# Fused attention and two MLPs on one core: first eight chunks of q and k in four groups of two, tau and the first weight pieces asked for later

## The chip, the cores and the metric

One core of one Trainium2 chip. The metric is device time in microseconds (us) of one execution. The kernel before takes 1052.99 us (median of 3 runs, 1052.94 to 1054.34). The engines are called as in the profile: PE (TensorE), DVE (VectorE), ACT (ScalarE), POOL (GpSimd) and SP, which here only asks for transfers.

## The reference

```python
qn = q / (norm(q, axis=1) + 1e-6)          # q, k, v: 1 x 6080 x 256
kn = k / (norm(k, axis=1) + 1e-6)
s  = kn.T @ qn / tau                       # 256 x 256
a  = softmax(s, axis=-1)
x  = v @ a                                 # 6080 x 256
h  = x @ w_in;  g = max(0.01 * h, h);  x = g @ w_out
h  = x @ w2_in; g = where(h >= 1, h, where(h <= -1, 0, (h + 1)**2 / 4))
out = g @ w2_out                           # w_in 256 x 2048, w_out 2048 x 256
```

[...]

## The kernel before

**Stage 1 (the loop over `groups`, lines 353 to 384)** reads q and k once, in groups of 128-row chunks: two groups of two chunks, ten of four, one of two, and a rest of 2 x 96 rows. Per group SP asks for q and for k (line 357), PE adds the group's part of kn.T @ qn into PSUM (`s_matmuls`, line 350: four matmuls of 256 columns per chunk pair, that is two per chunk), ACT squares both tiles and DVE adds the squares into `accq` and `acck` (line 373; the first two groups are squared straight into the two halves of the accumulators, line 368, and need no add). For the last four groups (`HELD`) PE takes one half of the columns at once and the other half after the loop. Then come the norms (`nq`, `nk`), the softmax and its transposes.

**The weights** come in 32 *pieces* of 512 KB, in the order of `pieces`: w_in 0, w_in 1, w_out 0, w_in 2, w_out 1, and so on. `load_pieces` asks for one; `LOAD_AT` names the groups of stage 1 after which one more is asked for, by ACT's queue. `decode_piece` turns float64 bits into float32: ACT makes the magnitude (`magnitude`, line 180), DVE works on it (lines 193, 195, 198, 202, 206) and adds the parts (210, 213 or 229). From w_in 2 and w_out 0 on, ACT then copies the sum into a rounded high part (lines 220, 237) and DVE subtracts for the low part (217, 233).

**The order of the work** is written out by hand. `decode_piece` is a generator: `pump(n)` takes as many of its steps as `n` credits pay for, between other instructions. What ACT has to do for a piece isn't issued by the generator: it is put on a list (`later`), and `flush()` issues that list. Inside stage 1 there are a flush and a pump per tile; a piece isn't touched before two groups after the one it was asked for (`loaded_at[i] + 2 > group[0]`). Behind stage 1 `FLUSH` and `PUMP` give the places, in slots of one PE product:

```python
PUMP = [..., ((0.8, 2.4, 3.9, 5.4, 6.6, 8.6, 10.0), 2.6), ((1.4, 2.8, 5.4, 6.9, ...), 2.6)]
FLUSH = [..., (0.5, 2.0, 3.5), (0.5, 1.4, 4.4, 5.3, 11.8, 14.8, 15.7)]
```

The second entries hold for the first eighth of the first layer, which lasts 10.5 slots; the third for the other seven. So the flushes there are at slots 0.5, 2.0, 3.5 and then at 10.5 + 0.5 = 11.0.

**Stage 2, the first layer's first pair of column blocks**, uses the weights as they get ready. In eighth j, PE multiplies x by the product wx of softmax and w_in j (tile `ph`, lines 331 to 333: high x high, low x high, high x low), ACT takes the leaky relu `c` (600) and rounds it to `gh` (618), DVE makes `gl` (623), and PE multiplies by w_out j (tile `acc`, reads `l2w`, high part in 331, low part in 332). One `wps` product per eighth makes the next wx from `et` and w_in j + 1 (reads `w1i`: high part in 331 and 332, low part in 333). PE, ACT and DVE each run their instructions in the order issued.

**Transfers**: a transfer signals one of eight semaphores (DMAHW0 to 7) that go round among all transfers of SP and ACT. Whoever asks with a number waits until the transfer that had that number last has landed.

Of the kernel before, what the change touches and what calls it, by code (L numbers as in the profile page):

```python
# [11 lines left out]
AF = mybir.ActivationFunctionType  # L12
# [10 lines left out]
CPG = 4  # L23
WARM = 8
HELD = 4


A11, A22, A12, S1, S2, S3, S4 = range(7)
# [33 lines left out]
        ((3, 6.0), (4, 6.0), (5, 6.0), (6, 6.0), (7, 6.0), (7, 10.9), (7, 16.0))]  # L62


LOAD_AT = (1, 2, 4, 8)
FOLD = 12

PLAIN_W = 2

# [7 lines left out]
def xcit_moe_moe(ctx, tc, q, k, vT, tau, w_in, w_out, w2_in, w2_out, outT):  # L77
# [10 lines left out]
    nc = tc.nc  # L88
    V, G, A = nc.vector, nc.gpsimd, nc.scalar
# [36 lines left out]
    def flush():  # L126

        while later:
            later.pop(0)()

    def load_pieces(n, dma):

        while len(raws) < min(n, len(pieces)):
            nm, j = pieces[len(raws)]
            if nm[-1] == "o":
                src = weights[nm].rearrange("(k p) c w -> p k c w", p=P)[:, 2 * j:2 * j + 2]
            else:
                src = weights[nm].rearrange("(k p) f w -> p k f w", p=P)[:, :, 256 * j:256 * (j + 1)]
            raw = dec.tile([P, 2, 256, 2], U32, tag="raw", name="raw", bufs=3)
            dma.dma_start(out=raw, in_=src)  # L140
            loaded_at[len(raws)] = group[0]
            raws.append(raw)
# [130 lines left out]
    def pump(n):  # L273
        nonlocal credit
        credit = min(credit + n, 2 * n)
        while credit > 0:
            c = next(prep)
            if c == 100:
                break
            credit -= c  # L280
# [24 lines left out]
    half, tiny, dummy = (const.tile([P, 1], F32, name=nm) for nm in ("half", "tiny", "dummy"))  # L305
    ones = const.tile([P, P], F32, name="ones")
    ident = const.tile([P, P], F32, name="ident")
    tau_sb = const.tile([P, 1], F32, name="tau_sb")
# [4 lines left out]

    groups = []
    t0 = 0
    for s in [2, 2] + [CPG] * 10 + [2]:
        groups.append((t0, P, s))
        t0 += P * s
    groups.append((t0, (N - t0) // 2, 2))
# [19 lines left out]
    for _ in range(WARM):  # L339
        nc.tensor.matmul(out=warm, lhsT=ones, rhs=ones, start=True, stop=True)  # L340

    A.activation(out=dummy, in_=tiny, func=AF.Sqrt)
    nq = ps_h.tile([P, NB], F32, tag="h", name="nq")[:, :C]
    nk = ps_h.tile([P, NB], F32, tag="h", name="nk")[:, :2 * KC].rearrange("p (c t) -> p c t", c=KC)
    tiles = []
# [1 line left out]
    def s_matmuls(ic, gi):  # L347
        kt, qt, rows, s = tiles[gi]
        for i in range(s):
            nc.tensor.matmul(out=s_ps[ic], lhsT=kt[:rows, i, ic * P:(ic + 1) * P], rhs=qt[:rows, i, :],  # L350
                             start=gi == 0 and i == 0, stop=gi == len(groups) - 1 and i == s - 1)

    for gi, (t0, rows, s) in enumerate(groups):
        tl = []
        for src, nm in ((q, "q"), (k, "k")):
            t = ep.tile([P, CPG, C], F32, tag=nm, name=nm)
            nc.sync.dma_start(out=t[:rows, :s, :], in_=src[t0:t0 + rows * s, :].rearrange("(p s) c -> p s c", s=s))
            tl.append(t)
        if gi == 0:
            nc.sync.dma_start(out=tau_sb, in_=tau)  # L360
        qt, kt = tl
        tiles.append((kt, qt, rows, s))
        s_matmuls(0, gi)
        if gi < len(groups) - HELD:
            s_matmuls(1, gi)
        for t, a in ((qt, accs[0]), (kt, accs[1])):
            if gi < 2:
                A.activation(out=a[:, 2 * gi:2 * gi + 2, :], in_=t[:, :s, :], func=AF.Square)
            else:
                sq = ep.tile([P, CPG, C], F32, tag="sq", name="sq", bufs=4)  # L370
                A.activation(out=sq[:rows, :s, :], in_=t[:rows, :s, :], func=AF.Square)
                if gi < FOLD:
                    V.tensor_add(out=a, in0=a, in1=sq)
                else:
                    for i in range(0, s, 2):
                        V.tensor_add(out=a[:rows, 0:2, :], in0=a[:rows, 0:2, :], in1=sq[:rows, i:i + 2, :])
            if gi == FOLD - 1:
                V.tensor_add(out=a[:, 0:2, :], in0=a[:, 0:2, :], in1=a[:, 2:4, :])
            flush()
            if gi < len(groups) - 4:  # L380
                pump(S_PUMP)
        group[0] = gi
        if gi in LOAD_AT:
            load_pieces(min(len(raws) + 1, decoded[0] + 3), A)
    xr = load_x(0, 0, nc.sync)
# [2 lines left out]

    for gi in range(len(groups) - HELD, len(groups) - HELD + 2):
        s_matmuls(1, gi)  # L390
    for i in range(2):
        nc.tensor.matmul(out=nq, lhsT=ones, rhs=accs[0][:, i, :], start=i == 0, stop=i == 1)
    for ic in range(KC):
        for i in range(2):
            nc.tensor.matmul(out=nk[:, ic], lhsT=accs[1][:, i, ic * P:(ic + 1) * P], rhs=ones[:, :2], start=i == 0, stop=i == 1)
    for gi in range(len(groups) - HELD + 2, len(groups)):
        s_matmuls(1, gi)
# [274 lines left out]
    for i, (m, p, j) in enumerate(quads):  # L672
# [7 lines left out]
        t = base  # L680
# [21 lines left out]
        if m == 0:  # L702
            k = 0 if not first else 2 if i else 1
# [4 lines left out]
        if j == 0 and i + NQ < len(quads):  # L708
            nm, np_, _ = quads[i + NQ]
# [9 lines left out]
    for k in range(4 * KC):  # L719
        t = base + 2 + k  # L720
# [35 lines left out]
```

## Time and profile before

| what | value |
|---|---|
| runs | 1054.34, 1052.99, 1052.94 us |
| profiled execution, first to last instruction (span) | 1052.2 us; no other time of it is given |
| PE / DVE / ACT busy | 99% / 77% / 80% |
| granted clock of PE, mean | 1.000 |
| stage 1, from the first S matmul to the norms | 4.27 to 47.06 us |
| first product with w_out 0 | 65.70 us |

A row of the timeline has start, duration, engine, line, operation, written tile <- read tiles, and in brackets how long the engine had been idle and what ended it. A float32 matmul is two records. Times are microseconds from the start of the span.

### The profile page before, as it was taken

What the parts mean: (1) busy time and instruction counts of PE and PEld (TensorE: products, weight loads), DVE (VectorE), ACT (ScalarE), POOL (GpSimd) and SP (SyncE); (2) the same over time, 40 slices, a digit from 0 to 9 for tenths busy, and PEclk for the clock granted to TensorE, in tenths of its full rate; (3) what the DMA queues carried; (4) which work ended last, traced back from release to release, by engine and by line L of the source; (5) the groups of instructions that cost most, each with busy time, mean ns of one, the idle gap of its engine ahead of it and who ended that gap; (6) DMA issues with size and microseconds to landing.
All of it is one profiled execution on the core that took longest, in us unless ns stands there. A gap on an engine that the chain in (4) does not pass through costs nothing.

```text
span 1052.2 us, 13435 instructions
## 1 busy us (share of the span) xinstructions
PE 1042.1 (99%) x4676; PEld 870.3 (83%) x4676; DVE 814.6 (77%) x1366; ACT 837.0 (80%) x1437; POOL 0.9 (0%) x9
## 2 busy tenths in 40 slices
PE   8999999999999999999999999999999999999998
PEld 7888878888888887888888888888888888888887
DVE  5989887678778778876547779779778878878765
ACT  6677777777787777777668888888888888888886
POOL 0000000000000000000000000000000000000000
PEclk9999999999999999999999999999999999999999
DMA  9645465448759569556446445436435444543531
GB/s 355 240 168 165 158 250 200 165 160 295 256 196 329 181 229 319 204 202 223 150 165 208 145 152 204 165 115 224 157 136 196 159 165 168 185 147 129 205 140 63
DMA packets 54164, 201.82 MB, mean 192 GB/s; under 512 B 5520, under 2 KB 6544, under 8 KB 54096
## 3 DMA queue, kind: packets, MB, share of 16 engines
q1 hardware_dynamic: 53008, 198.86, 53.9%
q10 hardware_dynamic: 1088, 2.10, 0.5%
q8 instruction: 37, 0.61, 0.2%
q14 instruction: 31, 0.25, 0.1%
HBM read 163.32 MB, written 37.62 MB: 191 GB/s over the span
## 4 chain that ended last, share of the span: by engine, by line
PE 95%; DMA 2%; DVE 1%; ACT 1%; issue 0%; SPq 0%; DVEq 0%
PE acc L332 16%; PE acc L333 16%; PE acc L331 16%; PE pX L331 7%; PE pX L332 7%; PE pX L333 7%; PE pW L331 4%; PE pW L333 4%; PE pW L332 4%; PE s_ps L350 4%; PE pY L332 2%; PE pY L333 2%; PE pY L331 2%; PE ph L332 1%; PE ph L331 1%; PE ph L333 1%
## 5 line engine op out<-in xcount | busy, mean ns | idle before, releaser
L623 DVE TENSOR_TENSOR gl<-c,gh 128x512 fp32r<-128x512 f32 (+1 forms) x384 | 261.0, 680 | 65.7 <-ACT gh L618 65.1
L332 PE MATMUL acc<-gh,l2w 128*128 128x512 f32 (+1 forms) x768 | 297.6, 387 | 0.2 <-DVE l2w L233 0.2
L331 PE MATMUL acc<-gh,l2w 128*128 128x512 f32 (+1 forms) x768 | 297.5, 387 | 0.0
L333 PE MATMUL acc<-gl,l2w 128*128 128x512 f32 (+1 forms) x768 | 297.5, 387 | 0.0
L618 ACT CAST gh<-c 128x512 fp32r<-128x512 f32 (+1 forms) x384 | 234.9, 612 | 5.3 <-DVE c L614 0.8
L332 PEld LDWEIGHTS acc<-gh,l2w 128*128 128x128 f32 x768 | 144.1, 188 | 28.9 <-DVE l2w L233 0.5
L331 PEld LDWEIGHTS acc<-gh,l2w 128*128 128x128 f32 x768 | 144.1, 188 | 28.8 <-ACT l2w L237 0.3
L333 PEld LDWEIGHTS acc<-gl,l2w 128*128 128x128 f32 x768 | 144.1, 188 | 28.6
L331 PE MATMUL pX<-xo,l1w 128*128 128x512 f32 (+1 forms) x352 | 136.3, 387 | 1.2 <-ACT s L583 1.2
L605 ACT ACTIVATE u<-c,half 128x512 f32<-128x512 f32 (+1 forms) x144 | 103.8, 721 | 42.1 <-DVE c L591 42.0
L332 PE MATMUL pX<-xo,l1w 128*128 128x512 f32 (+1 forms) x352 | 136.3, 387 | 0.0
L333 PE MATMUL pX<-xo,l1w 128*128 128x512 f32 (+1 forms) x352 | 136.2, 387 | 0.0
L583 ACT COPY s<-pX 128x512 f32<-128x512 f32 (+1 forms) x176 | 101.6, 577 | 30.1 <-PE pX L333 30.1
L608 ACT ACTIVATE u<-u 128x512 f32<-128x512 f32 (+1 forms) x192 | 120.6, 628 | 1.3
L600 ACT ACTIVATE c<-c 128x512 f32<-128x512 f32 (+1 forms) x120 | 75.2, 627 | 55.8 <-DVE c L591 55.5
L591 DVE TENSOR_TENSOR c<-pY,s 128x512 f32<-128x512 f32 (+1 forms) x88 | 60.2, 684 | 61.8 <-PE pY L333 57.1
L614 DVE SCALAR_TENSOR_TENSOR c<-u,c 128x512 f32<-128x512 f32 (+1 forms) x144 | 98.1, 681 | 10.6 <-ACT u L608 10.6
L591 DVE TENSOR_TENSOR c<-pW,s 128x512 f32<-128x512 f32 (+1 forms) x88 | 60.3, 685 | 39.3 <-PE pW L333 28.6
L591 DVE TENSOR_TENSOR c<-pX,s 128x512 f32<-128x512 f32 (+1 forms) x88 | 60.2, 684 | 24.3 <-PE pX L333 20.8
L331 PEld LDWEIGHTS pX<-xo,l1w 128*128 128x128 f32 x352 | 66.1, 188 | 14.8 <-ACT s L583 1.6
L332 PEld LDWEIGHTS pX<-xo,l1w 128*128 128x128 f32 x352 | 66.1, 188 | 13.1
L333 PEld LDWEIGHTS pX<-xo,l1w 128*128 128x128 f32 x352 | 66.1, 188 | 13.1
(123 smaller groups left out, 1315.0 us busy)
## 6 DMA issues: line engine op xcount, KB each, us to landing
l1w<-l1d SPq DMA_DIRECT2D x80, 896.0 KB, 4.6
l2w<-l2d SPq DMA_DIRECT2D x88, 512.0 KB, 5.1
raw<-in_w_out_dram SPq DMA_DIRECT2D x15, 512.0 KB, 5.9
l1d<-l1w SPq DMA_DIRECT2D x8, 896.0 KB, 4.4
l1d<-l1s SPq DMA_DIRECT2D x8, 896.0 KB, 5.3
raw<-in_w_in_dram SPq DMA_DIRECT2D x13, 512.0 KB, 6.1
q<-in_q_dram SPq DMA_DIRECT2D x10, 512.0 KB, 8.0
k<-in_k_dram SPq DMA_DIRECT2D x10, 512.0 KB, 9.1
```

The costliest lines, as they stand in the source:

```text
L331: nc.tensor.matmul(out=out, lhsT=wh, rhs=mh, start=first, stop=False, skip_group_check=skip)
L332: nc.tensor.matmul(out=out, lhsT=wl, rhs=mh, start=False, stop=False, skip_group_check=skip)
L333: nc.tensor.matmul(out=out, lhsT=wh, rhs=ml, start=False, stop=last, skip_group_check=skip)
L350: nc.tensor.matmul(out=s_ps[ic], lhsT=kt[:rows, i, ic * P:(ic + 1) * P], rhs=qt[:rows, i, :], start=gi == 0 and i == 0, stop=gi == len(gro ...
L583: A.copy(out=s[i], in_=bank["W" if i == "5" else "X"])
L591: V.tensor_tensor(out=tile_c(r), in0=bank[name], in1=s[i], op=ALU.add)
L600: A.activation(out=c[r], in_=src, func=AF.Prelu, alpha=0.01)
L605: A.activation(out=u[r], in_=source(r), func=AF.Relu, scale=0.5, bias=half[:, 0:1])
L608: A.activation(out=u[r], in_=u[r], func=AF.Square)
L614: V.scalar_tensor_tensor(out=c[r], in0=u[r], scalar=1.0, in1=src, op0=ALU.min, op1=ALU.max)
L618: A.copy(out=g[int(r[0]), int(r[1])][0], in_=c[r])
L623: V.tensor_tensor(out=lo, in0=c[r], in1=hi.bitcast(F32), op=ALU.subtract)
```

## The change

Stage 1 now has four groups of two chunks at its start (`SMALL`) and nine of four; its groups are numbered one higher from there on, and the place where the accumulators are folded (`FOLD`) moves with them. Groups 2 and 3 are squared into a tile and added by DVE in halves of the accumulators. ACT asks for the first k, SP for all else of q and k. tau is asked for by ACT after group 3 and no longer by SP after the first k. The square-root call that loads ACT's table stands after the squares of group 0. The first four weight pieces are asked for after groups 3, 4, 6 and 9 of the new count, in place of 1, 2, 4 and 8: in chunks read by then, 8, 12, 20 and 32 in place of 4, 8, 16 and 32.

```diff
+SMALL = 4
-LOAD_AT = (1, 2, 4, 8)
-FOLD = 12
+LOAD_AT = (3, 4, 6, 9)
+FOLD = 13
-    for s in [2, 2] + [CPG] * 10 + [2]:
+    for s in [2] * SMALL + [CPG] * 9 + [2]:
-    A.activation(out=dummy, in_=tiny, func=AF.Sqrt)
-            nc.sync.dma_start(out=t[:rows, :s, :], in_=src[...])
+            (A if gi == 0 and nm == "k" else nc.sync).dma_start(out=t[:rows, :s, :], in_=src[...])
-        if gi == 0:
-            nc.sync.dma_start(out=tau_sb, in_=tau)
-                if gi < FOLD:
+                if gi < SMALL:
+                    V.tensor_add(out=a[:, 2 * gi - 4:2 * gi - 2, :], in0=a[:, 2 * gi - 4:2 * gi - 2, :], in1=sq[:, 0:2, :])
+                elif gi < FOLD:
                     V.tensor_add(out=a, in0=a, in1=sq)
+        if gi == 0:
+            A.activation(out=dummy, in_=tiny, func=AF.Sqrt)
         group[0] = gi
+        if gi == LOAD_AT[0]:
+            A.dma_start(out=tau_sb, in_=tau)
         if gi in LOAD_AT:
             load_pieces(min(len(raws) + 1, decoded[0] + 3), A)
```

What moves, in three places. First, ACT behind stage 1: `w` and `wx` are the scaled product of softmax and w_in and its rounded copy, `raw` a piece, `c` and `gh` the first layer's result and its rounded copy, `eh` the rounded softmax. Before:

```order
L180 ACTIVATE a<-raw 128x512
L237 CAST l2w<-a 128x512
L468 ACTIVATE w_542<-wps,sums 128x256 x2
L473 CAST wx<-w_542 128x512
L600 ACTIVATE c<-ph 128x512
L503 CAST eh<-et 128x512
```

With the change (its lines are numbered one to four higher):

```order
L477 CAST wx<-w_543 128x512
L604 ACTIVATE c<-ph 128x512
L507 CAST eh<-et 128x512
L622 CAST gh<-c 128x512
L604 ACTIVATE c<-ph 128x512
L622 CAST gh<-c 128x512
L604 ACTIVATE c<-ph 128x512
L181 ACTIVATE a<-raw 128x512
L238 CAST l2w<-a 128x512
L181 ACTIVATE a<-raw 128x512
```

The copy of w_out 0 into `l2w` stood ahead of the first `c`; now it stands behind the third `c` and a magnitude.

Second, DVE behind stage 1 (`xs`, used below, is a sum for the next pair's x). Before, from the rest of piece w_out 0 to its low part:

```order
L202 TENSOR_SCALAR e<-a 128x512
L206 SCALAR_TENSOR_TENSOR raw<-raw,e 128x512
L229 TENSOR_TENSOR a<-a,raw 128x512
L193 TENSOR_SCALAR a<-a 128x512
L195 TENSOR_SCALAR a<-a 128x512
L233 TENSOR_TENSOR l2w<-a,l2w 128x512
```

With the change, from that low part on, to the low part of the next piece, w_in 2:

```order
L234 TENSOR_TENSOR l2w<-a,l2w 128x512
L199 SCALAR_TENSOR_TENSOR a<-raw,a 128x512
L627 TENSOR_TENSOR gl<-c,gh 128x512
L203 TENSOR_SCALAR e<-a 128x512
L207 SCALAR_TENSOR_TENSOR raw<-raw,e 128x512
L627 TENSOR_TENSOR gl<-c,gh 128x512 x2
L214 TENSOR_TENSOR a<-a,raw 128x512
L658 TENSOR_TENSOR xs<-xr 128x512
L194 TENSOR_SCALAR a<-a 128x512
L196 TENSOR_SCALAR a<-a 128x512
L218 TENSOR_TENSOR w1i<-a,w1i 128x512
```

The first three operations on piece w_out 0 (193, 195, 198) stood in stage 1 and stand behind it now. The low part `l2w` comes right after the first two operations on piece w_in 2 in both; these two wait for the second of the two magnitudes in the list of ACT. Behind `l2w`, eleven operations now end with the low part of w_in 2, and three `gl` and an `xs` that stood behind that low part stand ahead of it. PE's own order is the same in both kernels.

Third, SP's last transfers of stage 1, with what they wait for. Before:

```order
L357 DMA q<-in_q_dram 128x512 [waits DMAHW5_49,PE_49,Activation_49]
L357 DMA k<-in_k_dram 128x512 [waits DMAHW6_49,DMAHW1_49,Activation_49]
L357 DMA q<-in_q_dram 96x512 [waits DMAHW7_49,PE_49,Activation_49]
L357 DMA k<-in_k_dram 96x512 [waits DMAHW0_49,Activation_49]
L297 DMA xr<-in_vT_dram 128x2x1024 [waits DMAHW1_49]
```

With the change:

```order
L357 DMA q<-in_q_dram 128x512 [waits DMAHW7_49,PE_49,Activation_49]
L357 DMA k<-in_k_dram 128x512 [waits DMAHW2_49,DMAHW0_49,Activation_49]
L357 DMA q<-in_q_dram 96x512 [waits DMAHW1_49,PE_49,Activation_49]
L357 DMA k<-in_k_dram 96x512 [waits DMAHW2_49,Activation_49]
L298 DMA xr<-in_vT_dram 128x2x1024 [waits DMAHW3_49]
```

The transfer that had the number before is the fourth weight piece for `xr` (DMAHW1) before, and for the last k (DMAHW2) with the change.

## Rows read from the trace of the kernel before

Times are in us from the start of the span.

**Rows 1.** The page, part 1: busy time, share and instructions.

```profile
PE 1042.1 (99%) x4676; PEld 870.3 (83%) x4676; DVE 814.6 (77%) x1366; ACT 837.0 (80%) x1437; POOL 0.9 (0%) x9
```

**Rows 2.** The chain that ended last, in order of time: start, duration, what.

```profile
10.09 7.14 PE s_ps L350 x32
17.32 29.74 PE s_ps L350 x136
47.06 0.88 PE nq L392 x4
```

**Rows 3.** Timeline, 0 to 30 us: start, duration, engine, line, operation.

```profile
0.73 1.28 ACT L342 ACT_TABLE_LOAD   x1 [0.73 <-PEq L744]
...
4.27 1.89 PE L350 MATMUL s_ps<-q,k 128*128 128x256 f32 x8
...
7.26 1.96 PE L350 MATMUL s_ps<-q,k 128*128 128x256 f32 x8 [1.10 <-DMA k<-in_k_dram]
...
10.09 20.20 PE L350 MATMUL s_ps<-q,k 128*128 128x256 f32 x91 [0.86 <-DMA k<-in_k_dram]
```

**Rows 4.** Stretches: from:to length, POOL busy, granted clock, DMA share, GB/s.

```profile
3.50:3.75 0.25, 0.00 (x0) 1.00 0.80 91
...
5.50:5.75 0.25, 0.00 (x0) 1.00 1.13 352
...
8.75:9.00 0.25, 0.00 (x0) 1.00 1.01 410
```

**Rows 5.** Transfers at the end of stage 1, timeline, and q's landing times.

```profile
29.66 0.40 ACTq L140 DMA_DIRECT2D raw<-in_w_in_dram  x1
...
33.43 0.32 SPq L357 DMA_DIRECT2D k<-in_k_dram  x1
...
37.69 0.39 SPq L297 DMA_DIRECT2D xr<-in_vT_dram  x1
...
42.47 4.18 PEld L350 LDWEIGHTS s_ps<-q,k 96*128 96x128 f32 x20 [0.28 <-DMA k<-in_k_dram]
...
DMA to landing us min/median/max: 2.5/8.0/10.4
```

**Rows 6.** Timeline, the last add of the squares on DVE.

```profile
46.19 0.68 DVE L376 TENSOR_TENSOR acck<-acck,sq 96x512 f32<-96x512 f32 x1
```

**Rows 7.** Timeline, ACT behind stage 1.

```profile
60.53 0.62 ACT L237 CAST l2w<-a 128x512 fp32r<-128x512 f32 x1 [2.38 <-DVE a L229]
...
65.19 0.59 ACT L600 ACTIVATE c<-ph 128x512 f32<-128x512 f32 x1
...
66.24 0.61 ACT L220 CAST w1i<-a 128x512 fp32r<-128x512 f32 x1
66.75 0.66 ACT L180 ACTIVATE a<-raw 128x512 f32<-128x512 f32 x1
```

**Rows 8.** Timeline, PE in the first layer.

```profile
65.70 0.39 PE L331 MATMUL acc<-gh,l2w 128*128 128x512 f32 x1
65.92 0.39 PE L332 MATMUL acc<-gh,l2w 128*128 128x512 f32 x1
...
69.11 0.28 PE L331 MATMUL wps<-w1i,eh 128*128 128x256 f32 x1
...
69.35 0.28 PE L333 MATMUL wps<-w1i,eh 128*128 128x256 f32 x1
...
81.45 0.28 PE L331 MATMUL wps<-w1i,eh 128*128 128x256 f32 x1
```

**Rows 9.** Timeline, DVE in the first layer.

```profile
67.44 0.43 DVE L193 TENSOR_SCALAR a<-a 128x512 f32<-128x512 f32 x1 [0.79 <-ACT a L180]
...
68.24 0.69 DVE L217 TENSOR_TENSOR w1i<-a,w1i 128x512 fp32r<-128x512 f32 x1
68.85 0.69 DVE L623 TENSOR_TENSOR gl<-c,gh 128x512 fp32r<-128x512 f32 x1
```

**Rows 10.** Waits of PE from 57 us on: total, times, longest.

```profile
PE pX L331 <- ACT s L583: 1.2, 1, 1.2
```

More of the change, by code (lines that the diff above doesn't have):

```diff
@@ L356, in xcit_moe_moe @@
             t = ep.tile([P, CPG, C], F32, tag=nm, name=nm)
-            nc.sync.dma_start(out=t[:rows, :s, :], in_=src[t0:t0 + rows * s, :].rearrange("(p s) c -> p s c", s=s))
+            (A if gi == 0 and nm == "k" else nc.sync).dma_start(out=t[:rows, :s, :], in_=src[t0:t0 + rows * s, :].rearrange("(p s) c -> p s c", s=s))
             tl.append(t)
-        if gi == 0:
-            nc.sync.dma_start(out=tau_sb, in_=tau)
         qt, kt = tl
```

## The prediction, made before the changed kernel was run

> **What bounds the kernel now.** I read the busy times first: PE is busy for 99% of the span [rows 1], so the time changes only by what PE waits for, or stops waiting for. The chain that ended last shows where stage 1 stands on PE: a stretch that starts at 10.09, one that starts at 17.32 and runs without a break for 29.74 us, then the norms at 47.06 [rows 2]. So whatever stage 1 can still win lies ahead of 17.32. From 57 us to the end PE waits 1.2 us in one place and next to nothing elsewhere [rows 10]. Two questions follow: how much earlier stage 1 ends, and whether the later first layer still finds its weights ready.
>
> **What the waits ahead of 17.32 cost.** The stretch of 29.74 us holds 136 records [rows 2], 0.2187 us each. Eight records are 1.75 us, so the first group, started at 4.27, would let the second start at 6.02; it started at 7.26, waiting for k [rows 3]: 1.24 lost. The next would start at 9.01 and started at 10.09 [rows 3]: 1.08. Then 32 records are 7.00 and the following start was 7.23 later [rows 2]: 0.23. In all 2.55 us, the most that stage 1 can give.
>
> **The change part by part.**
>
> *Groups of two, tau and weights later: the front of stage 1.* The queue moves 91 GB/s in the quarter from 3.50 and 410 later [rows 4], just where tau's tiny transfer stood between k and the second q; and weights shared the queue from early on. With tau and weights behind eight chunks the first groups should come in time for PE. I count the full 2.55 as won at the front. ACT's asking for the first k changes nothing here: PE's first group starts when its warm-up ends.
>
> *Its price on ACT and DVE.* A square as the first activation and the square root after it make a second table load, 1.28 us like the one at 0.73 [rows 3]; ACT has only eight short squares until PE needs nothing from it, so I cost it at nothing. If that cover went, the squares would be late for DVE. DVE gets four adds of 128x512 for two of 128x1024, some 0.3 us more, and loses three operations on piece w_out 0, 0.43 + 0.43 + 0.69 [rows 9], from stage 1. DVE ended stage 1 at 46.87 [rows 6], just ahead of PE's norms [rows 2]; it can end 1.2 earlier. So it sets no bound under a win of about 1.2.
>
> *The tail of stage 1.* PE reached the last group at 42.69 (17.32 plus 116 records, of the 136 all but the last 20), when its k had just landed: the weight load waited 0.28 until 42.47 [rows 5]. With 2.55 won, PE wants this k at 40.14. But its issue now waits for the fourth weight piece, as `xr` did before. That piece was asked for at 29.66 and let `xr` go at 37.69 [rows 5], 8.0 later; it is again asked for after 32 chunks, so I take 37.7 as the issue, in place of 33.43 [rows 5]. A q transfer took 2.5 us at the least and 8.0 in the median [rows 5]. 2.5 gives 40.2, hence a win of 2.5; 42.5, as before, gives 0.2; half a microsecond later than that a loss of 0.3. By then the queue holds little else, so I take 4.3, nearer to the least than to the median: a landing at 42.0, and a win of **0.7**. The Trainium skill, "DMA: Bandwidth & Descriptors" (Anatomy of one DMA), fits a transfer by 2.0 us plus its bytes over 436 GB/s; for these 192 KB that is an estimate of 2.5 us, the landing at 40.2 and a win of 2.5, and the whole sum below would be 1.8 lower. No row shows such a transfer alone at that place.
>
> *The first w_out piece, high part.* From here on I take the clock of the kernel before, as if stage 1 ended alike, and add the lateness. Before, ACT copied w_out 0 at 60.53 [rows 7], five microseconds ahead of PE's first use at 65.70 [rows 8]. With the change the piece enters stage 2 three operations behind; its sum isn't ready at the flush of slot 3.5, and the next flush is at 11.0. So the copy stands behind the third `c` (65.19) and a magnitude: the place that the copy of w_in 2 had, 66.24 to 66.85 [rows 7]. PE waits from 65.70 to 66.88: **1.2**.
>
> *Its low part.* DVE must first do two short operations on the next piece, and these wait for ACT's second magnitude, at 66.75 [rows 7]. The same pair stood at 67.44 behind the same magnitude, and the low part of w_in 2 behind it, at 68.24 to 68.93 [rows 9]. Now the low part of w_out 0 has that place. PE reads it in the second matmul, at 65.92 before [rows 8]; that becomes 68.95, 3.03 late, **1.85** more.
>
> *The next piece, w_in 2.* PE's product `wps` comes at 69.11 [rows 8], now 72.14. Behind 68.24 DVE has a mask operation, `gl`, a short one, a product, two `gl` and the sum of w_in 2. A long one starts 0.61 after the one before (68.24 to 68.85), a short one takes about 0.4 (two, 67.44 to 68.24, take 0.80) [rows 9]: the sum starts near 72.3 and ends at 73.0, ACT's copy takes 0.61 [rows 7], PE starts at 73.65: **1.5**. The low part comes after `xs` and two short ones, 74.3 to 75.0. PE reads it in the third matmul, 0.24 after the first [rows 8], 73.9: **1.1**. Together 5.65.
>
> *The product after that* follows 12.34 us behind the first (69.11 to 81.45) [rows 8], so PE wants its low part at 87.3. Counted in DVE's new order, 14 long and 6 short operations lie between: 14 x 0.61 + 6 x 0.4 = 10.9, from 74.3 on: done at 85.9 if DVE never waits for ACT. Before, the same stretch had some 0.8 us of such waits, and PE's late products now cause more. Between 0 and 1.2; I take **0.6**. After that the pieces have caught up, since PE is six microseconds behind its old clock and DVE is not.
>
> *Sum:* 1.2 + 1.85 + 1.5 + 1.1 + 0.6 - 0.7 = **+5.55 us**. The profiled span of 1052.2 becomes 1057.75; the runs' median, 1052.99, lies 0.8 above that span, and the same offset gives **1058.5 us**.
>
> **Bounds.** Stage 1 between -2.5 and +0.3; the four waits on the pieces between 5.0 (each could shrink a little, as DVE gains when PE waits) and 5.65, and the fifth between 0 and 1.2. A wait of 1.85 us is longer than any on PE ahead of 17.32, so something that follows it and that no row here shows can't be excluded; I allow 1.0 for it, as much as the wait of the second group before. Ends: 1052.99 + 5.0 - 2.5 = 1055.5 and 1052.99 + 5.65 + 1.2 + 0.3 + 1.0 = 1061.1.
>
> **The rivals.**
>
> *The front's win stays and the pieces aren't late: not slower, about 1051.* The place is ACT's copy of w_out 0. If ACT and DVE behind the softmax ran 3 us ahead of where I put them, no wait would come, and 1.2 to 2.5 of stage 1 would stay: 1051 to 1052. For it: ACT is idle for 2.38 just ahead of that copy [rows 7]. Against: this idle time ended before the third `c`, and `c` is made from a PE product, so the copy can't run ahead of PE. It would decide from 65.7 on the old clock. 0.05.
>
> *Half the waits: about 1055.* PE's first wait gives DVE and ACT time, and if the magnitude of w_in 2 were made in that time, the low part and w_in 2 would be nearly ready: 3.0 - 0.7 leaves 1055.3. Against: the magnitude stands behind the copy on ACT and the sum behind three `gl` on DVE, in that order. 0.12.
>
> *Short transfers slow stage 1: about 1059.6.* While the groups of two were moved, the queue reached 352 GB/s, against 410 with groups of four [rows 4]. Another four chunks of each of q and k, 1.05 MB, would cost 1.05/0.352 - 1.05/0.410 = 0.4 us, and with the late last k stage 1 ends 0.4 late, not 0.7 early: 5.65 + 0.6 + 0.4 = +6.65, 1059.6. The Trainium skill, "DMA: Bandwidth & Descriptors" (Rules for kernel authors), asks for 1 MiB or more per transfer and for merging small ones; the rows go the same way. 0.2.
>
> **How the numbers follow.** The forecast has 0.63, the rivals 0.05, 0.12 and 0.2. Less than 0.2%, or 2.1 us, is not told from no change. The first rival gives 0.03 of faster and 0.02 of same; the second lies on the bound of 1055.1 and gives 0.07 of same. Faster 0.03, same 0.09, slower 0.88. The range takes the bounds above, 1055.5 to 1061.1; one in ten lies under it.
>
> **What would show it.** PE's first S groups start at 4.27, 6.0, 7.8 and 9.5 without waits. SP asks for the last k just after the fourth piece landed. The first `acc` matmul waits about 1.2 us for ACT and the second about 1.9 for DVE, the first and the third `wps` matmul 1.5 and 1.1. The forecast is wrong if `l2w` is copied ahead of the third `c`, or if stage 1 ends over 2 us earlier or later than 47.06.

## The result, and the profile after

The changed kernel takes 1060.78 us (median of 4 runs, 1059.68 to 1062.35), the kernel before 1053.43 (4 runs, 1052.94 to 1054.34): ratio 1.0066, 95% interval 1.0053 to 1.008. It is slower, as forecast; 1060.78 lies near the upper end of the range given (1055.5 to 1061.1), 2.3 above the 1058.5 predicted, and two of the four runs lie above that end. The profiled execution took 1059.82 with a span of 1058.0, 5.8 more than the span of before.

First, what PE waits for, over the whole of the changed kernel (total, times, longest), against the single wait behind 57 us of [rows 10]:

```profile
PE acc L333 <- DVE l2w L234: 1.8, 2, 1.6
...
PE wps L334 <- DVE w1i L218: 1.1, 2, 0.9
PE acc L332 <- ACT l2w L238: 1.0, 1, 1.0
...
PE s_ps L350 <- DMA k<-in_k_dram: 1.0, 2, 0.5
PE wps L332 <- ACT w1i L221: 0.5, 1, 0.5
```

Four new rows stand there, on the two halves of w_out 0 (`l2w`) and of the w_in pieces (`w1i`: w_in 2, and the low part of the piece after it once more); of the 1.8 on the low part of `l2w`, 0.2 come at a later piece. The wait of PE on `s` is gone. In the timeline of PE they are these matmuls (start, duration, and in brackets the wait):

```profile
66.77 0.50 PE L332 MATMUL acc<-gh,l2w 128*128 128x512 f32 x1 [1.03 <-ACT l2w L238]
...
68.85 0.50 PE L333 MATMUL acc<-gh,l2w 128*128 128x512 f32 x1 [1.58 <-DVE l2w L234]
...
74.42 0.39 PE L332 MATMUL wps<-w1i,eh 128*128 128x256 f32 x1 [0.50 <-ACT w1i L221]
...
75.14 0.39 PE L334 MATMUL wps<-w1i,eh 128*128 128x256 f32 x1 [0.23 <-DVE w1i L218]
...
88.61 0.39 PE L334 MATMUL wps<-w1i,eh 128*128 128x256 f32 x1 [0.87 <-DVE w1i L218]
```

The same matmuls started at 65.70, 65.92, 69.11 and 69.35 before [rows 8], and the last at 81.86:

```profile
81.86 0.39 PE L333 MATMUL wps<-w1i,eh 128*128 128x256 f32 x1
```

PE's order is the same in both kernels, so the difference of starts tells how late PE is there: 1.07, 2.93, 5.31, 5.79 and 6.75 us.

What ACT did around the first of them:

```profile
65.06 0.59 ACT L604 ACTIVATE c<-ph 128x512 f32<-128x512 f32 x1
65.56 0.65 ACT L181 ACTIVATE a<-raw 128x512 f32<-128x512 f32 x1
66.10 0.61 ACT L238 CAST l2w<-a 128x512 fp32r<-128x512 f32 x1
66.61 0.66 ACT L181 ACTIVATE a<-raw 128x512 f32<-128x512 f32 x1
```

And DVE, whose low part of `l2w` stands behind two operations that wait for the last of these:

```profile
61.33 0.69 DVE L230 TENSOR_TENSOR a<-a,raw 128x512 f32<-128x512 f32 x1
...
67.30 0.43 DVE L194 TENSOR_SCALAR a<-a 128x512 f32<-128x512 f32 x1 [1.37 <-ACT a L181]
67.77 0.43 DVE L196 TENSOR_SCALAR a<-a 128x512 uint32<-128x512 uint32 x1
68.11 0.68 DVE L234 TENSOR_TENSOR l2w<-a,l2w 128x512 fp32r<-128x512 f32 x1
```

The sum of w_out 0 was ready at 62.02 (61.33 + 0.69), and its copy started at 66.10: four microseconds in which the data lay there and ACT's order had other things first.

Between the second and the third wait stands something that is no wait. Stretches of PE (from:to, length, then busy time of PE, PEld, DVE, ACT and POOL, the granted clock, DMA share, GB/s):

```profile
66.00:69.40 3.40, 1.05 (x3) 0.67 (x4) 2.06 (x5) 3.40 (x8) 0.00 (x0) 1.00 0.00 0
69.40:72.80 3.40, 3.40 (x9) 2.65 (x8) 3.37 (x7) 0.97 (x2) 0.00 (x0) 0.50 0.89 301
```

From 66.00 to 69.40, the stretch with the first two waits, PE was busy for 1.05 us; from 69.40 to 72.80 the granted clock is 0.50 (1.2 of 2.4 GHz). Eight matmuls from 69.42 to 72.82 take 0.43 each in place of 0.23, 1.6 us more.

Last, stage 1. The chain that ended last (start, duration, what), to be held against [rows 2]:

```profile
9.43 9.00 DMA raw<-in_w_in_dram
...
18.93 7.58 DMA k<-in_k_dram
...
29.26 7.96 DMA raw<-in_w_in_dram
...
37.28 4.95 DMA k<-in_k_dram
42.23 0.14 issue
42.37 4.56 PE s_ps L350 x20
46.93 0.88 PE nq L396 x4
```

PE ran its first 96 records without a wait, from 4.57 on, waited at 26.64 for a k (0.55) and at 42.37 for the last k (0.42). The norms are at 46.93, 0.13 earlier than the 47.06 of before. (The timeline, in which matmuls overlap, has the same two starts at 46.76 and 46.90; the experiments below are read from the timeline.) Both late k were asked for only after a weight piece had landed.

### The profile page after: what moved, and what is told of

It is laid out like the page before. It is cut to its first block, busy times and chain, and to the rows that moved or that the text cites. A ratio compares the mean times of both kernels' runs of the same rounds, so it can differ in the third digit from the quotient of the medians.

```text
span 1058.0 us, 13444 instructions
## 1 busy us (share of the span) xinstructions
PE 1045.2 (99%) x4676; PEld 871.7 (82%) x4676; DVE 816.3 (77%) x1368; ACT 837.8 (79%) x1439; POOL 0.9 (0%) x9
## 4 chain that ended last, share of the span: by engine, by line
PE 92%; DMA 4%; ACT 2%; DVE 1%; issue 1%; SPq 0%; DVEq 0%; ACTq 0%
PE acc L333 16%; PE acc L334 16%; PE acc L332 16%; PE pX L333 7%; PE pX L332 7%; PE pX L334 7%; PE pW L332 4%; PE pW L333 4%; PE pW L334 4%; PE pY L333 2%; PE pY L332 2%; PE pY L334 2%; DMA raw<-in_w_in_dram 2%; DMA k<-in_k_dram 1%; PE ph L333 1%; PE ph L332 1%
```

## The experiments

All were timed beside the kernel before on the same chip; its median was 1053.6 to 1054.2 there. A ratio is time over that of before.

### Which part of the change makes the loss

**Pieces alone.** The kernel before with one line changed:

```diff
-LOAD_AT = (1, 2, 4, 8)
+LOAD_AT = (2, 3, 5, 8)
```

> The kernel before with one line changed: the four weight pieces asked for after 8, 12, 20 and 32 chunks, as in the changed kernel; tau, the first k and the groups stay as they were. My theory (the later pieces alone make the loss): PE waits about 1.0 us for the copy of w_out 0 into l2w on ACT, about 1.6 us for its low part on DVE, 0.5 to 2 us at the next two products with w_in, and runs some 3.4 us at half clock behind them; 5 to 7 us slower than before, ratio 1.005 to 1.0065. Rival (the short groups and the moved tau make the loss): no wait at l2w, within 0.2% of before.

Measured: 1060.56 us, ratio 1.0056 (1.0041 to 1.0071). Waits of PE from 57 to 100 us:

```profile
PE wps L333 <- DVE w1i L217: 1.7, 2, 0.9
PE acc L332 <- DVE l2w L233: 1.6, 1, 1.6
PE wps L331 <- ACT w1i L220: 1.3, 1, 1.3
PE acc L331 <- ACT l2w L237: 1.0, 1, 1.0
```

The whole loss is there with the groups, tau and the first k as before; the half clock came later in this execution, within 74 to 80 us.

**Everything but the pieces.** The changed kernel, pieces as before:

```diff
-LOAD_AT = (3, 4, 6, 9)
+LOAD_AT = (1, 3, 5, 9)
-        if gi == LOAD_AT[0]:
+        if gi == 3:
             A.dma_start(out=tau_sb, in_=tau)
```

> The changed kernel with the four weight pieces back after 4, 8, 16 and 32 chunks; groups of two, tau by ACT after group 3, first k by ACT stay. My theory: the copy into l2w stands ahead of the first c again, no wait of PE on l2w or w1i, no half clock; the time falls to that of the kernel before or up to 1.5 us under it (1051.5 to 1053.5), the gain being what is left of stage 1's 2.5 us. Rival (short groups and moved tau make the loss): stays 5 us or more above before.

Measured: 1051.92 us, ratio 0.9979 (0.997 to 0.9989). No wait on `l2w` or `w1i`. Stage 1 gained nothing in this trace, though: PE's norms started at 47.37, after 0.5 us of waiting for DVE's last adds. Five operations on w_out 0 stood inside stage 1 there, two more than before; that they made the adds late is likely and not shown.

**The groups of two alone**, the price of short transfers (`SMALL`, `FOLD` and the adds of groups 2 and 3 as in the change):

```diff
...
-    for s in [2, 2] + [CPG] * 10 + [2]:
+    for s in [2] * SMALL + [CPG] * 9 + [2]:
...
-LOAD_AT = (1, 2, 4, 8)
+LOAD_AT = (1, 3, 5, 9)
```

> The kernel before with the groups of two alone (four of them, pieces after the same 4, 8, 16 and 32 chunks, tau and all of q and k by SP as before). It prices the short transfers, the third rival of the prediction. My theory: they cost little, stage 1 ends within 0.5 us of before, total within 0.1% of before. Rival: the queue moves less in short transfers and stage 1 ends 0.4 us or more later, with the last k landing later than 42.5 us.

Measured: 1052.21 us, ratio 0.9984 (0.9975 to 0.9994). The norms started at 47.29, 0.4 later than the 46.90 of the first trace, of which 0.3 is a later start of PE's first S matmul; the total is no longer. So the 0.4 us of my third rival isn't seen in the time. The Trainium skill, "DMA: Bandwidth & Descriptors" (Rules for kernel authors), asks for 1 MiB or more per transfer; going from 512 KB to 256 KB for four more chunks cost nothing here that the ratio shows.

**tau alone**, asked for by ACT after group 1 of the kernel before:

```diff
-        if gi == 0:
-            nc.sync.dma_start(out=tau_sb, in_=tau)
...
+        if gi == LOAD_AT[0]:
+            A.dma_start(out=tau_sb, in_=tau)
```

> The kernel before with tau alone moved: asked for by ACT after group 1, ahead of the first weight piece, instead of by SP after the first k. My theory: the wait of 1.1 us at PE's second group falls under 0.5 us, part of it is lost again before the end of stage 1 as in the changed kernel, nothing moves behind stage 1; total 0 to 1.2 us faster than before. Rival (tau's place costs nothing, the queue's start is slow anyway): the second group starts at 7.0 or later as before.

Measured: 1053.26 us, ratio 0.9995 (0.9983 to 1.0006): no difference that can be told. The front did get better, PE reached its third group at 9.40 in place of 10.09, but the profiled execution, the slowest of its ten, then waited 2.23 us at 26.49 for a k that SP had asked for at 17.75 and that took 8.70 to land. In this execution the win at the front was not kept; its granted clock was also 0.50 from 58 to 60 us, behind the softmax.

### How the loss comes about

**One group earlier for one piece:**

```diff
-LOAD_AT = (3, 4, 6, 9)
+LOAD_AT = (2, 4, 6, 9)
-        if gi == LOAD_AT[0]:
+        if gi == 3:
             A.dma_start(out=tau_sb, in_=tau)
```

> The changed kernel with the first weight piece alone asked for one group earlier (groups 2, 4, 6 and 9, that is after 6, 12, 20 and 32 chunks; tau still after group 3). The three operations on w_out 0 are back in stage 1 and its copy is ahead of the first c. My theory (a missed place in a fixed order: all or nothing): no PE wait on l2w or w1i, no half clock, 1050.5 to 1053. Rival (the loss grows with each chunk of delay): half of the loss or more stays, 1056 or more.

Measured: 1052.44 us, ratio 0.9984 (0.9974 to 0.9993). The three other delays are still in, and yet all of the loss is gone: it is a step, not a slope, and it lies between 6 and 8 chunks for the first piece. ACT's copy is back at its old place:

```profile
60.40 0.62 ACT L238 CAST l2w<-a 128x512 fp32r<-128x512 f32 x1 [2.38 <-DVE a L230]
...
65.53 0.39 PE L332 MATMUL acc<-gh,l2w 128*128 128x512 f32 x1
```

**One more place for ACT's list.** The changed kernel with

```diff
-FLUSH = [..., (0.5, 2.0, 3.5), ...]
+FLUSH = [..., (0.5, 2.0, 3.5, 7.0), ...]
```

> The changed kernel with one more place at which ACT's list is issued, slot 7.0 of the first eighth, so that the copy of w_out 0 stands ahead of the first c; everything else as changed, the pieces as late as there. My theory (the loss is the place in ACT's order, not the landing of the pieces): the waits on l2w (1.0 and 1.6 us) and the half clock behind them go, w_in 2 is late by 1 us at the most; 1053 to 1055. Rival (the pieces themselves are late, whatever the order): PE waits as long at other places, time 1058 or more.

Measured: 1059.37 us, ratio 1.0047 (1.0032 to 1.0062). A miss. The copy did move ahead of the first `c` and the two waits on `l2w` went down to 0.2, but the next piece was then as late as ever. Waits of PE from 60 to 100 us:

```profile
PE wps L334 <- DVE w1i L218: 1.5, 1, 1.5
PE wps L332 <- ACT w1i L221: 0.8, 1, 0.8
PE ph L332 <- ACT c L604: 0.3, 1, 0.3
```

So the missed place explains the first two waits only. w_in 2 stays late: the 1.55 us of DVE's work on w_out 0 that left stage 1 (0.43 + 0.43 + 0.69) is still ahead of it. I had put it at 1 us late at the most; it was 2.3. This execution also had two stretches at half clock, within 54 to 60 and 74 to 80 us, and the first of them, behind the softmax, made PE late ahead of any piece: its first product with w_out 0 started at 67.87, 2.17 later than before, of which the end of stage 1 and a wait explain 0.4. So the total of this execution overstates what the added place left over.

**Is the half clock a loss of its own?** Ten products on constants fill PE's two waits at `acc`:

```diff
+FILL_ACC = (4, 6, 0)
...
-                mm3(a, w[:, 0, f, cs], w[:, 1, f, cs], gh, gl, ...)
...
+                    for i, (lhs, rhs) in enumerate(((w[:, 0, f, cs], gh), (w[:, 1, f, cs], gh), (w[:, 0, f, cs], gl))):
+                        for _ in range(FILL_ACC[i]):
+                            nc.tensor.matmul(out=other[:, :P], lhsT=ones, rhs=ones, start=True, stop=True)
+                        nc.tensor.matmul(out=a, lhsT=lhs, rhs=rhs, start=i == 0, stop=False)
```

> The changed kernel with ten 128-column products on constants put into PE's two waits at the first product with w_out 0 (four ahead of its first matmul, six ahead of its second; they write a bank that the next product clears), 1.0 and 1.5 us of them, so that PE is not idle there. Theory A (the loss is set by DVE's and ACT's order of the pieces, and the half clock only fills time in which PE would wait for w_in 2): the half clock of 69.4 to 72.8 us goes, the waits at the wps product grow from 0.7 to about 2 us, the time stays within 0.5 us of the changed kernel (1059 to 1061.5). Theory B (the half clock is a loss of its own): 1.5 us faster than the changed kernel, and the waits at wps stay at 0.7.

Measured: 1059.73 us, ratio 1.0053 (1.0034 to 1.0072), within the spread of the changed kernel. The clock behind the waits stayed at 1.00, and PE, arriving earlier, waited for w_in 2 instead (waits from 57 to 100 us; the lines are one higher here, and L534 is the filled product):

```profile
PE wps L335 <- DVE w1i L219: 1.7, 2, 0.9
PE wps L333 <- ACT w1i L222: 1.3, 1, 1.3
PE acc L534 <- DVE l2w L235: 0.3, 1, 0.3
```

That is 3.0 us on w_in against 1.6 in the changed kernel (0.5 + 0.23 + 0.87): 1.4 more, about the 1.6 that the half clock had taken. DVE's and ACT's order sets when `wps` starts; the half clock ran in time that PE would have waited. This execution, the slowest of its four, had a half clock elsewhere, behind the softmax (within 56 to 61 us), and its stage 1 ended 2.0 later than in the changed kernel's trace; so the total of this one trace tells nothing, and the waits do. The trace of the first experiment, pieces alone, bears them out: its half clock also came only later, and its waits on `w1i` are the same 1.7 and 1.3.

### What stage 1 hangs on

**The fourth piece a group later**, so that the last k's number is free:

```diff
-LOAD_AT = (3, 4, 6, 9)
+LOAD_AT = (3, 4, 6, 10)
```

> The changed kernel with the fourth piece asked for one group later (groups 3, 4, 6 and 10), so that the last k's issue no longer waits for that piece by its semaphore. My theory: SP asks for the last k before 35 us, the wait of 0.4 us at PE's last group goes, stage 1's norms start at 45.8 to 46.5 instead of 46.76; the waits behind stage 1 stay as they are; 0.3 to 0.9 us faster than the changed kernel. Rival (the last k is late because the queue is full): it lands as late as before and nothing changes.

Measured: 1060.55 us, ratio 1.0054 (1.0037 to 1.007). SP asked for the last k at 34.04, as expected, and yet PE got it no earlier:

```profile
34.04 0.32 SPq L357 DMA_DIRECT2D k<-in_k_dram  x1
...
43.47 4.56 PE L350 MATMUL s_ps<-q,k 96*128 96x256 f32 x20 [0.68 <-DMA k<-in_k_dram]
```

The rival was right. Asked for at 33.18, 33.43, 34.04, 37.28 and 38.29 (with the first piece earlier, before, here, changed, groups of two), the last k let PE start at 42.53, 42.47 (its weight load), 43.47, 42.37 and 42.90: issues five microseconds apart end within 1.1 us of each other, and not in their order. So the time of the issue doesn't set the landing. That the queue does fits the rows, and no run separates it: in the traces of before and changed the DMA engines are busy for 0.93 or more of every 2 us from 6 to 42.

How far a single trace carries here can be read from kernels with one and the same stage 1. The norms started at 46.76, 46.99, 46.99 and 48.79 in four traces of the changed one's (changed, the added place for ACT's list, both fillings of PE in the changed kernel) and at 46.90 and 48.04 in two of before's. A difference of a microsecond or two between two single traces there can be chance: the longer wait of this run, the 0.4 of the groups of two and the 0.13 of the changed kernel against before are all smaller. Within these traces a later issue of the last k goes with a later start (37.28, 37.57 and 39.81 with 42.37, 42.60 and 44.39), as it would if the whole queue ran late.

**The fourth piece behind the last k**, on the kernel with the first piece a group earlier:

```diff
-LOAD_AT = (2, 4, 6, 9)
+LOAD_AT = (2, 4, 6, 13)
```

> The kernel of the run before with the first piece one group earlier (groups 2, 4, 6), and the fourth piece asked for after group 13, behind nearly all of q and k. My theory now (the last k lands when the queue has moved all that was asked for by then, and a piece of 0.52 MB is 1.3 us of the queue at 405 GB/s): the last k lands near 41, the norms start 0.7 to 1.5 us earlier than in that run (46.92), nothing is late behind stage 1; 1050.8 to 1052. Rival (the last k's time is set by its issue and its own latency): norms at 46.5 or later, total as in that run, 1052.4.

Measured: 1051.73 us, ratio 0.9983 (0.9974 to 0.9992); PE's last group started earlier, and the norms at 46.13 in place of 46.92:

```profile
32.37 0.32 SPq L357 DMA_DIRECT2D k<-in_k_dram  x1
...
41.73 4.56 PE L350 MATMUL s_ps<-q,k 96*128 96x256 f32 x20 [0.53 <-DMA k<-in_k_dram]
46.13 1.03 PE L396 MATMUL nq<-accq,ones 128*128 128x256 f32 x4
```

Issued 0.8 earlier than there, with 0.52 MB less ahead of it, the last k let PE start 0.8 earlier, not the full 1.3 of the queue's time; in the time the two kernels can't be told apart. The kernel with the same stage 1 further down (ten products in the softmax) has the last k at 41.96 and the norms at 46.38. These are the two earliest ends of stage 1 in all fourteen traces, and the only two with a piece less ahead of the last k; against the spread above, two traces make that cause likely and don't show it.

### The spread of the runs

Half of the changed kernel's executions (two of four) were 2 us longer, at a clock of 0.996 in place of 0.997. PE idles 1.5 us in the softmax; five more products on constants fill all but 0.4 of that pause:

```diff
-FILL = (5, 3, 2)
+FILL = (10, 3, 2)
```

In the changed kernel:

> The changed kernel itself with ten in place of five products on constants in the softmax's pause, nothing else. Half of its executions had a clock of 0.996 and were 2 us longer than the others at 0.997. My theory: the longer ones had a second half-clock stretch behind the softmax; with PE filled all executions are like the short ones, 1058.5 to 1060, and the waits at l2w and wps and the half clock behind them stay. Rival (the longer ones come from elsewhere): runs of 1061 and more stay.

Measured: 1058.6 us, runs from 1058.07 to 1060.33, ratio 1.005 (1.0035 to 1.0065). No run of 1061 or more is left, though four runs are few. In its profiled execution the clock was 1.00 behind the waits at `acc` as well, with the same waits there, and longer ones on `w1i` (waits of PE from 57 to 100 us):

```profile
PE wps L334 <- DVE w1i L218: 1.7, 2, 0.9
PE acc L333 <- DVE l2w L234: 1.6, 1, 1.6
PE wps L332 <- ACT w1i L221: 1.3, 1, 1.3
PE acc L332 <- ACT l2w L238: 1.0, 1, 1.0
```

The `wps` matmul that is 6.75 late in the changed kernel was 6.78 late here:

```profile
88.64 0.39 PE L334 MATMUL wps<-w1i,eh 128*128 128x256 f32 x1 [0.87 <-DVE w1i L218]
```

Counted from each trace's own end of stage 1, that is 6.89 with the half clock and 6.69 without: it added 0.2 us at most there.

In the kernel with the fourth piece behind the last k:

> The same kernel with ten in place of five products on constants ahead of the softmax's transposes, where PE idles 1.5 us. It tests whether that pause is what drops the clock to half behind the softmax in some executions. My theory: no execution shows a granted clock under 0.999, the spread of the runs shrinks, the median is 0 to 0.6 us under that of the same kernel without. Rival (the pause has nothing to do with it): some executions at 0.998 as before, no difference.

Measured: 1050.79 us, ratio 0.9976 (0.9967 to 0.9985), the fastest of all, 11 runs within 1050.39 and 1051.39, none below a clock of 0.999. But the kernel without the five products, timed beside it, had none below 0.999 either (11 runs, median 1051.73). So this run can't say that the filling keeps the clock up, and its 0.9 us, more than the 0.6 I allowed, must come from something else, which stays open.

In the kernel before:

> The kernel before with ten in place of five products on constants in the softmax's pause. It asks two things. One: does before have the half clock behind the softmax in some executions, as the changed kernel has, so that filling the pause takes 0.3 to 1 us off its median (1052.7 to 1053.4)? Two: is the wait of 1.23 us at 419.91 in its first trace regular? If ACT waits there for a piece in this execution too, it is, and explains 1.2 us by which kernels with other piece times beat before; if not, it was one execution's late transfer. Rival: no difference in the median, 1053.6 to 1053.9.

Measured: 1052.58 us, ratio 0.9988 (0.9978 to 0.9997). None of 11 executions was below 0.999; of the unfilled kernel's 14 beside it five were at 0.998. And the wait of 1.23 us at 419.91 [rows 10] was not there: ACT's magnitude waited for its piece 0.6 us here and 2.83 in the first trace.

```profile
416.59 0.67 ACT L180 ACTIVATE a<-raw 128x512 f32<-128x512 f32 x1 [0.60 <-DMA raw<-in_w_out_dram]
```

It isn't the first trace's alone, though. ACT waits for this piece in 11 of the 14 traces, and PE behind it in three. In the changed kernel with the pause filled:

```profile
424.51 0.66 ACT L181 ACTIVATE a<-raw 128x512 f32<-128x512 f32 x1 [2.65 <-DMA raw<-in_w_out_dram]
425.70 0.50 PE L332 MATMUL pX<-xo,l1w 128*128 128x512 f32 x1 [1.04 <-ACT s L587]
```

In the kernel with the fourth piece behind the last k they are 1.92 and 0.32. Each time PE waits 1.6 us less than ACT, and where ACT waits up to 1.64, PE waits for nothing there. So it is a place with 1.6 us of room, at which the piece comes now early, now late, with the first pieces early and with them late.

## Why the prediction was right, and where it was off

The mechanism behind stage 1 was right, place by place; the one at the end of stage 1 was not. PE's lateness grew by these steps (starts after minus starts before, each less the one ahead of it):

| step | predicted | measured |
|---|---|---|
| end of stage 1 | -0.7 | -0.13 |
| high part of w_out 0 | 1.2 | 1.2 |
| low part of w_out 0 | 1.85 | 1.86 |
| w_in 2, high part | 1.5 | 2.4 |
| w_in 2, low part | 1.1 | 0.5 |
| next product | 0.6 | 1.0 |
| sum | 5.55 | 6.75 |

*The w_out steps* came out to a tenth, and for the reason given: the copy at 66.10 stood where the copy of w_in 2 had stood, the low part behind the second magnitude. The one-line experiment on the kernel before and the one with the first piece moved show it from both sides. The added place for ACT's list shows what the order of ACT alone is worth: it took away these two waits and not the loss, since DVE's three operations still came late.

*The w_in 2 steps* are 2.86 together against 2.6, split otherwise: PE was slowed by the half clock, which I had allowed for in the bound as "something that follows it and that no row here shows" and not in the sum; so it reached `wps` late and waited less there. Filling PE showed that this shifts time between the two and adds 0.2 us at most.

*The front and the tail.* The front's 2.55 came: no wait before 26.64 (PE started 0.3 later at 4.57). Two late transfers took it back, of which I had one. The last k, put at a landing of 42.0, let PE start at 42.37, 0.9 later than its records ask for. The other is a wait of 0.55 in the middle (1.1 us later than its 96 records ask for, 4.57 + 96 x 0.2187 = 25.57), after a k that SP could ask for only at 18.93, behind a weight piece: I looked for such issues at the last k alone. The reason that I gave for the tail, the number held by the fourth piece, is the step that failed: without it the last k landed no earlier. "By then the queue holds little else" was wrong, and so was the least time of a transfer as an end. What the runs show in its place is a last k that lets PE start at 42.4 to 43.5 whether it is asked for at 33 or at 38; a queue that is still full is the likely cause, and taking a piece out ahead of it went with the two earliest ends. With one trace a kernel, the 0.7 and the 0.13 can't be told apart either. The fit of the Trainium skill, "DMA: Bandwidth & Descriptors" (Anatomy of one DMA), gives an estimate of 2.5 us from the issue to the landing; the page measured it on transfers asked for by GpSimd, and this k is asked for by SP. It doesn't agree with this trace: 4.95 us, and about 9 in the kernels that asked for it at 33 or 34.

*The level.* Of the 2.3 us between 1058.5 and 1060.78, little is in the span: 1057.75 was forecast, 1058.0 found. That is luck: two errors cancel there, the 1.2 of the sum and the 1.23 us at 419.91, which I took for part of the kernel; it is not in the trace after. In every run here that gives both, the time is 1.8 above the span; the median that I set beside the first span lies 0.8 above it. So that execution was 1 us longer than the median, and I carried the wrong offset over. The other 1.0 comes from the half of the executions that were 2 us longer, of which the four with the pause filled have none.

*The rivals.* "Half the waits" fell: nothing caught up. "Short transfers slow stage 1" fell with the groups of two alone, which were no slower. "Not slower" needed the pieces to be in time, and moving one of them by one group made the kernel not slower (1052.44); but of the front's win, which that rival kept, nothing was left at the end of stage 1 (46.92).

What beats both kernels: the changed one with the pieces after groups 2, 4, 6 and 13 and ten products in the softmax's pause, 1050.79 us. The pause alone gave 1.2 us on the kernel before by its ratio. The rest, pieces and groups, would be 1.2 by the difference of the ratios 0.9988 and 0.9976, whose intervals overlap; all 11 runs of the one lie below all 11 of the other, but they were not timed beside each other. Why the kernels with the pieces in time are some 0.2% faster than before, though stage 1 ends about as late, is settled only in part: none of 41 executions of those four kernels was at a clock under 0.999, against 25 of the 73 of before. That is the smaller part: the 48 executions of before at 0.999 or more have a median of 1053.4, all 73 one of 1053.8, and the four kernels lie at 1051.7 to 1052.4. Why they are spared stays open too. Their traces differ from before's in one thing in the softmax: behind the pause of 1.53, PE waits once more between two transposes before (0.18) and doesn't there; no run tests whether that matters.

## What to carry to other kernels

Where an order is written out by hand, a step that is delayed a little either keeps its place or loses a whole slot: look at which engine's place it falls to, and what stands ahead of it there, rather than at how much later its data comes. Work that leaves one stage has to be done in the next: here 1.55 us of DVE's work left stage 1 and turned up in front of the first product that needed it. And the last transfer of a saturated queue came no earlier for being asked for earlier; taking bytes out ahead of it is the thing to try. Before reading a microsecond out of one trace, read the same stretch in a trace of another kernel that shares it.

## What the runs showed of the hardware that was not expected

A pause of 1.5 us on PE in the softmax was followed, in some executions, by a stretch at a granted clock of 0.50 (within 54 to 60 us in the trace with the added place for ACT's list, where the first `wps` product took 3.38 us in place of 1.89). The trace with tau alone moved has such a stretch, and no other ahead of PE's end, at a mean of 0.998; by that mean which executions have it changes from run to run (25 of 73 of the kernel before are below 0.999). With products on constants in the pause, which cost no time that the runs show, all 11 executions of the kernel before were at 0.999 or above. The same waits at `acc` were followed by the half clock in two traces (changed, the fourth piece a group later) and not in two others (pieces alone, the changed kernel with the pause filled), so a single trace doesn't tell it.

One and the same late piece may cost PE 1.23 us in one execution and nothing in the next: ACT's wait for it was between none and 2.83 us in the 14 traces, and PE paid for what went beyond 1.6. A residual wait in a single trace should not be taken as the kernel's.
